# One row of w4 in a decode kernel: from the last POOL-queue load to four sync-queue loads on partitions 0 to 63

## The chip, the cores and the metric

The kernel runs on one core of a Trainium2 chip. The metric is the device time of one execution in microseconds: 211.09 us before the change, the median of three runs (210.95 to 211.11).

A core has five engines that run their own instruction streams: PE (TensorE, matmuls), DVE (VectorE), ACT (ScalarE), POOL (GpSimd) and SP (SyncE, which only issues DMAs here). Memory is moved by 16 DMA engines. A DMA that POOL issues goes through one queue, a DMA that SP issues through another; both queues are served by the same DMA engines. A load is cut into packets, and each DMA engine that takes part in a load signals its end.

## The reference

One decode step for four sequences (B = 4, one token each, D = 576) adds three things: the input `x`, attention over the last 2048 cached positions, and an MLP block. All inputs are bf16.

```python
xn = _layernorm(x)
out = x + attention(xn, k_cache, v_cache, wq, wo) + mlp(xn, w1, w2, w3, w4)

# attention: 32 query heads, 16 key heads, Dh 128, window W = 2048
q = (xn @ wq); scores = q k^T * Dh**-0.5; p = softmax(scores)
o = (p v) @ wo

# mlp, with one token per sequence: its shifted branch comes out as zero, so x1 = xn
h2 = gelu(_layernorm(x1) @ w3) @ w4          # w3 576 x 4608, w4 4608 x 576
mlp = x1 + h2
```

The branch through `w1` and `w2` shifts by one or two positions along a sequence of length one, so nothing but zeros is left of it; the kernel doesn't load those weights. What has to be read is mostly the cache: 16 loads of 4 MB (eight of K, eight of V), and about 20 MB of weights.

## The kernel before

**Loads.** `wq` comes first, on SP's queue, in two DMAs. All later big loads go through POOL's queue, in an order written out in `order` and issued by `flush_loads`: K and V tiles for eight head pairs (`load_kv`, indirect DMAs of 128 rows of 32 KB), `wo` in four quarters (`load_wo`), `w3` behind the second V tile, and at the very end the last quarter of `wo` and the whole of `w4` (`load_w4`). Three buffers hold K and V tiles; `free_one` issues the next load when a tile has been used up. `wq`, `w3` and `w4` follow one another in one buffer (tag "w", one buffer), so w4's tile can be written only after w3's last reader.

**Loop.** Each turn t of the main loop treats one pair of key heads: DVE turns the K tile (`k_transpose`, L297), PE makes scores (`k_scores`, L411), DVE and ACT do the softmax of the turn before, PE multiplies with V (`pv`, L475), and the head outputs are turned, summed and, every second turn, multiplied by a quarter of `wo` into the PSUM tile `acc` (`acc_matmuls`, L230). The program order of each engine is the order in the text of the kernel (`manual_schedule`).

**The MLP.** In turn t = 3 (`G_AT`) the first MLP product is made in between. `mlp_g(r)` for r = 0, 1, 2 multiplies the normalised input by column groups of w3 (L541) and copies the result from PSUM to SBUF (L545). The 4608 hidden values are kept as 36 columns of 128: hidden value e*2304 + p*18 + i stands on partition p in column e*18 + i. r = 0 and 1 make columns i = 0 to 15 of each half, r = 2 makes i = 16 and 17 of both. `mlp_turn(r)` brings the result to partitions with PE transposes (L554) and a DVE copy into `xs` (L560). `mlp_act` makes the tanh form of gelu on POOL and ACT (L564 to L569) and leaves it as bf16 in `gT`.

**The second MLP product.** w4 lies in the same way: partition p holds rows e*2304 + p*18 + i, 36 rows of 1,152 bytes. `load_w4` brings it in six pieces, `W4_PIECES = [0, 18, 25, 30, 34, 35, 36]`, that is 18, 7, 5, 4, 1 and 1 rows a partition. After the attention of the last head pair PE adds the pieces as they land, one pair of matmuls (two halves of 288 columns) for each row: the first two pieces into `acc` (L230), then the rest into two fresh PSUM tiles (`sum_open`, L244; `sum_matmuls`, L252), with the sum of `acc` added by `sum_fold` (L257). The result is cast by DVE (L719) and ACT (L721) and stored by SP (L722).

**PSUM tiles** of the pool `ps_m` (tag "m") rotate through two buffers: `g_ps` of r = 2, each `gT_ps`, the softmax sums `dn`, the spread heads `R` (read by ACT in `o_pick`, L521) and others take them in turn.

Of the kernel before, what the change touches and what calls it, by code (L numbers as in the profile page):

```python
# [22 lines left out]
def kernel(  # L23
# [14 lines left out]
    nc = tc.nc  # L38
    P = 128
    B, Sq, D = A_x.shape  # L40
# [4 lines left out]
    F = B_w3.shape[1]  # L45
# [3 lines left out]
    NF = F // P  # L49
    NFH = NF // 2  # L50
    NPR = Hkv // 2
    NJ = B * rep
    QD = 32
# [24 lines left out]
    wp = ctx.enter_context(tc.tile_pool(name="w", bufs=1))  # L78
# [4 lines left out]
    const = ctx.enter_context(tc.tile_pool(name="const", bufs=1))  # L83
# [3 lines left out]
    ps_m = ctx.enter_context(tc.tile_pool(name="ps_m", bufs=2, space=PSUM))  # L87
# [3 lines left out]
    w_tiles = {}  # L91
# [61 lines left out]
        nc.gpsimd.dma_start(out=t[:, KJ * F:], in_=B_w3[KJ * P:D, :].rearrange("r (e f) -> (r e) f", e=2))  # L153
        w_tiles["w3"] = t

    W4_PIECES = [0, NFH, NF - 11, NF - 6, NF - 2, NF - 1, NF]

    def load_w4():
        t = wp.tile([P, NF, D], BF16, tag="w", name="w4_sb")
        src = B_w4.rearrange("(e p i) n -> e p i n", e=2, p=P)  # L160
        for lo, hi in zip(W4_PIECES, W4_PIECES[1:]):
            e, at = divmod(lo, NFH)
            nc.gpsimd.dma_start(out=t[:, lo:hi, :], in_=src[e][:, at:at + hi - lo, :])  # L163
        w_tiles["w4"] = t

    order = [("K", 0), ("K", 1)]
    for t in range(NPR):
# [31 lines left out]
    ident_f = ident_w[:, 0:P]  # L199
# [15 lines left out]
    ln2T = cleared([P, KJ + 2, QD], "ln2T")  # L215
    ZP = (NSL - 1) * NJ
    qz = cleared([P, ZP + NPR * 4 * P], "qz")
    gT = const.tile([P, NF, B], BF16, name="gT")
    op = const.tile([P, WOR, B], BF16, name="op")

    acc = ps_acc.tile([P, CW], F32, name="acc")
# [5 lines left out]
    def acc_matmuls(terms):  # L227
        for k, (lhsT, rhs) in enumerate(terms):
            for i in range(NI):
                nc.tensor.matmul(out=acc_of(k % 2 * NI + i), lhsT=lhsT, rhs=rhs[:, i * CW:(i + 1) * CW],  # L230
                                 start=False, stop=False, skip_group_check=True)
# [17 lines left out]
    def sum_matmuls(terms, first=False):  # L249
        for k, (lhsT, rhs) in enumerate(terms):  # L250
            for i in range(NI):
                nc.tensor.matmul(out=sum_of(i), lhsT=lhsT, rhs=rhs[:, i * CW:(i + 1) * CW],  # L252
                                 start=first and k == 0, stop=False, skip_group_check=True)
# [48 lines left out]
    for kb in range(NQD):  # L302
        nc.gpsimd.tensor_copy(out=sel[:, :, :, kb, :],
                              in_=ident_bf[:].rearrange("p (ib i e) -> p ib e i", ib=2, e=2))
# [23 lines left out]
    for g in range(2):  # L328
        nc.gpsimd.tensor_copy(out=same_j[:, g * 2 * QD:(g + 1) * 2 * QD].rearrange("p (e s j) -> p e s j", e=2, j=NJ),
                              in_=sel_j[:].unsqueeze(2).to_broadcast([P, 2, NSL, NJ]))  # L330
# [177 lines left out]
    def o_spread(h):  # L508
        if h % WOQ < WOQ - 1:
            return  # L510
        x = st.pop("ox")
        R = ps_m.tile([P, B, WOR], F32, tag="m", name="R")
        for b in range(B):
            nc.tensor.matmul(out=R[:, b, :], lhsT=x[:, b].rearrange("p h d -> p (h d)"), rhs=sel_i[:],
                             start=True, stop=True)
        st["R"] = R
# [9 lines left out]
        acc_matmuls([(op[:, i, :], wo_tiles[h // WOQ][:, i, :]) for i in range(WOR)])  # L526

    G_CHUNKS = [(e, 4 * g, 4) for e in range(2) for g in range(NQD)] + [(e, 16, 2) for e in range(2)]
    xs = const.tile([P, NF, B], F32, name="g_x")
    g_sb = {}  # L530

    def mlp_g(r):
        w3 = w_tiles["w3"]
        chunks = G_CHUNKS[r * NQD:(r + 1) * NQD]
        n = chunks[0][2]
        g_ps = (ps_o if r < 2 else ps_m).tile([P, P, n], F32, tag="O" if r < 2 else "m", name="g_ps")
        for j in range(KJ + 1):
            for g, (e, i0, _) in enumerate(chunks):
                base, k = (j * F + e * (F // 2), j) if j < KJ else (KJ * F, KJ + e)
                cols = w3[:, base:base + F // 2].rearrange("p (q i) -> p q i", q=P)  # L540
                nc.tensor.matmul(out=g_ps[g * QD:(g + 1) * QD], lhsT=ln2T[:, k, :], rhs=cols[:, :, i0:i0 + n],  # L541
                                 start=(j == 0), stop=False, skip_group_check=True)
        m = len(chunks) * QD
        g_sb[r] = bigp.tile([P, P, n], F32, tag="g", name="g_sb", bufs=1)
        nc.scalar.activation(out=g_sb[r][0:m], in_=g_ps[0:m], func=ACT.Copy)  # L545

    def mlp_turn(r):
        chunks = G_CHUNKS[r * NQD:(r + 1) * NQD]
        n, m = chunks[0][2], len(chunks)
        gT_all = ps_m.tile([P, n * m, QD], F32, tag="m", name="gT_ps")  # L550
        gT_ps = gT_all[:].rearrange("p (u g) x -> p u g x", u=n)
        gs = g_sb.pop(r)
        for u in range(n):
            nc.tensor.transpose(out=gT_ps[:, u].rearrange("p g x -> p (g x)"), in_=gs[0:m * QD, :, u],  # L554
                                identity=ident_f[0:m * QD, 0:m * QD])
        if r < 2:
            dst = xs[:, r * NFH:r * NFH + 16, :].rearrange("p (g u) b -> p u g b", u=n)
        else:
            dst = xs[:].rearrange("p (g c) b -> p c g b", c=NFH)[:, 16:18]
        nc.vector.tensor_copy(out=dst, in_=gT_ps[:, :, :, 0:B])  # L560

    def mlp_act():
        u = const.tile([P, NF, B], F32, name="g_u")
        nc.gpsimd.tensor_tensor(out=u[:], in0=xs[:], in1=xs[:], op=ALU.mult)  # L564
        nc.gpsimd.tensor_scalar(out=u[:], in0=u[:], scalar1=GELU_A, scalar2=1.0, op0=ALU.mult, op1=ALU.add)
        nc.gpsimd.tensor_tensor(out=u[:], in0=u[:], in1=xs[:], op=ALU.mult)
        nc.scalar.activation(out=u[:], in_=u[:], func=ACT.Tanh, scale=GELU_C)
        nc.gpsimd.tensor_scalar(out=u[:], in0=u[:], scalar1=0.5, scalar2=0.5, op0=ALU.mult, op1=ALU.add)
        nc.gpsimd.tensor_tensor(out=gT[:], in0=u[:], in1=xs[:], op=ALU.mult)  # L569

    def mlp_terms(lo, hi):
        w4 = w_tiles["w4"]
        return [(gT[:, u, :], w4[:, u, :]) for u in range(lo, hi)]


    G_AT = 3
# [1 line left out]
    for t in range(NPR - 1):  # L578
        a, o = t - 1, t - 2
        if a >= 0:  # L580
            sm_max(a, 1)
        if o >= 0:
            o_scale(o)
        k_transpose(t, 1)
        if t == G_AT:
            mlp_g(0)
        k_mask(t, 0)
        k_scores(t, 0, 0)
        if a >= 0:
# [12 lines left out]
        k_scores(t, 1, 0)  # L602
        if o >= 0:
            o_turn(o)
        k_scores(t, 1, 1)
        if a >= 0:
            sm_turn(a, 0)
        if o >= 0:
            o_sum(o)
            o_expand(2 * o + 1)  # L610
        k_transpose(t, 3)
        free_one()
        if a >= 0:
            sm_turn(a, 1)
        if t == G_AT:
            mlp_g(2)
            mlp_turn(1)
        k_mask(t, 1)
        k_scores(t, 2, 0)
        if a >= 0:  # L620
            sm_den(a)
            sm_rec(a)
            pv(a, 0, 0, SC // 2)
        k_scores(t, 2, 1)
        sm_max(t, 0)
        if o >= 0:
            o_spread(2 * o + 1)
        if a >= 0:
            pv(a, 0, SC // 2, SC)
        if o >= 0:  # L630
            o_pick(2 * o + 1)
        if t == G_AT:
            mlp_turn(2)
            mlp_act()
        if t + 1 < NPR:
            k_transpose(t + 1, 0)
        k_scores(t, 3, 0)
        if a >= 0:
            pv(a, 1, 0, SC // 2)
        k_scores(t, 3, 1)  # L640
        if a >= 0:
            pv(a, 1, SC // 2, SC)
            free_one()
        if o >= 0:
            o_proj(2 * o + 1)
# [57 lines left out]
    o_sum(hl)  # L703
    o_expand(2 * hl + 1)
    o_spread(2 * hl + 1)
    acc_matmuls(mlp_terms(*W4_PIECES[0:2]))
    o_pick(2 * hl + 1)
    o_proj(2 * hl + 1)
    acc_matmuls(mlp_terms(*W4_PIECES[1:3]))
    half = sum_open()  # L710
    sum_matmuls(mlp_terms(*W4_PIECES[2:4]), first=True)
    sum_fold(half)
    sum_matmuls(mlp_terms(W4_PIECES[3], NF))

    fin = const.tile([B, D], out.dtype)
    for i in range(NI):
        dst = fin[:, i * CW:(i + 1) * CW]
# [35 lines left out]
```

## Time and profile before

| what | us |
|---|---|
| median of 3 runs | 211.09 (210.95 to 211.11) |
| the profiled execution, its own time | 210.85 |
| its span, first to last instruction | 209.1 |
| PE busy | 144.0 (69%) |
| DVE busy | 124.3 (59%) |
| POOL busy, ACT busy | 31.6, 28.5 |
| POOL's queue, time of its packets | 91.7% of 16 engines' span, 82.45 MB |
| SP's queue, time of its packets | 5.5%, 4.72 MB |

Issues and landings of the loads around the change:

```profile
w_sb<-in_B_w_dram POOLq DMA_DIRECT2D x1, 1008.0 KB, 30.6
w_sb<-in_B_w_dram POOLq DMA_DIRECT2D x1, 720.0 KB, 31.9
...
w_sb<-in_B_w_dram POOLq DMA_DIRECT2D x2, 144.0 KB, 28.6
```

Each line names the tile and the tensor, the issuing queue, how many DMAs, the size of one and the median microseconds from issue to landing. The two single-row pieces of w4 are the two of 144 KB.

The profile's "busy" counts what an engine executes. The chain of waits goes back from the last instruction: at each step to what released it, or to the instruction before it on the same engine. A DMA on that chain means that an engine stood waiting for data at that point. The trace also holds each DMA packet (queue, start, duration, size), and for each load the times at which DMA engines signalled its end.

### The profile page before, as it was taken

How to read it: one execution, taken by the hardware profiler on the slowest of the kernel's cores; microseconds unless marked ns; L12 is line 12 of the kernel's file. 1: busy time of each engine (PE TensorE's matmuls, PEld its weight loads, DVE VectorE, ACT ScalarE, POOL GpSimd, SP SyncE). 2: the span in 40 equal slices, each digit the busy share in tenths (PEclk: the TensorE clock that was granted, in tenths of full speed). 3: DMA queues.
4: the chain of work that ended last, by engine and by line, in shares of the span. 5: the costliest groups of instructions: out<-in, count | busy, mean ns of one | idle time of the engine just before them, and what ended most of it. 6: DMA issues, size and time to landing. Idle time of an engine off the chain costs nothing.

```text
span 209.1 us, 2165 instructions
## 1 busy us (share of the span) xinstructions
PE 144.0 (69%) x878; PEld 57.7 (28%) x878; DVE 124.3 (59%) x174; ACT 28.5 (14%) x64; POOL 31.6 (15%) x63
## 2 busy tenths in 40 slices
PE   0248198649669933069996793677959947986974
PEld 0013133223214310014432431133314312432442
DVE  5510679993199600098908991998099818896220
ACT  6102500100102011003001201020102010204010
POOL 5680001003200110000133011001010152100000
PEclk9999669997979995559999999696997995899699
DMA  8999999999999999999999999999999999999991
GB/s 302 401 439 464 401 433 429 464 401 433 470 397 437 447 429 407 407 471 445 407 442 453 401 439 423 464 401 439 464 401 428 442 433 407 445 451 404 420 404 60
DMA packets 4155, 87.32 MB, mean 418 GB/s; under 512 B 488, under 2 KB 496, under 8 KB 1200
## 3 DMA queue, kind: packets, MB, share of 16 engines
q0 software_dynamic: 3840, 82.45, 91.7%
q1 hardware_dynamic: 296, 4.72, 5.5%
q8 instruction: 7, 0.11, 0.2%
q14 instruction: 4, 0.03, 0.0%
q10 hardware_dynamic: 8, 0.00, 0.0%
HBM read 87.17 MB, written 0.00 MB: 417 GB/s over the span
## 4 chain that ended last, share of the span: by engine, by line
DMA 63%; PE 18%; DVE 14%; POOL 2%; issue 2%; ACT 0%; DVEq 0%; POOLq 0%
DMA kn<-in_A_k_cache_dram,row 47%; DMA w_sb<-in_B_w_dram 16%; PE S L411 10%; DVE kt L297 9%; PE O L475 6%; DVE mx L417 1%; POOL w_sb L163 1%; DVE pt L456 1%; PE sum L252 1%; PE S L399 0%; POOL vn L125 0%; PE oT L486 0%; DVE dm L420 0%; POOL rstd L268 0%; POOL wo_sb L147 0%
## 5 line engine op out<-in xcount | busy, mean ns | idle before, releaser
L297 DVE STREAM_TRANSPOSE kt<-kn 128x2048 int32<-128x2048 int32 x32 | 73.6, 2304 | 48.7 <-DMA kn<-in_A_k_cache_dram,row 46.1
L411 PE MATMUL S<-kt,qz 128*128 128x512 bf16 x256 | 78.1, 438 | 33.6 <-DVE kt L297 33.6
L411 PEld LDWEIGHTS <-qz 128*128 128x128 bf16 x256 | 23.5, 104 | 72.5 <-issue 55.8
L475 PE MATMUL O<-vn,pt 128*64 128x512 bf16 x256 | 36.4, 415 | 6.5 <-DMA vn<-in_A_v_cache_dram,row 5.3
L456 DVE STREAM_TRANSPOSE pt<-E 64x512 bf16<-64x512 bf16 x32 | 22.1, 690 | 1.2 <-ACT E L447 0.9
L125 POOL DMA_INDIRECT vn<-in_A_v_cache_dram,row x8 | 7.7, 960 | 92.9 <-DVE kt L297 88.4
L447 ACT ACTIVATE E<-S,bias 128x512 bf16<-128x512 f32 x16 | 10.9, 683 | 75.9 <-DVE bias L440 75.9
L475 PEld LDWEIGHTS <-pt 128*64 128x64 bf16 x256 | 13.5, 116 | 23.3 <-issue 13.9
L125 POOL DMA_INDIRECT kn<-in_A_k_cache_dram,row x8 | 7.9, 989 | 41.5 <-PE O L475 22.7
L480 ACT ACTIVATE O_sb<-O,rd 128x512 f32<-128x512 f32 x8 | 5.5, 688 | 54.5 <-PE O L475 54.5
L417 DVE TENSOR_REDUCE mx<-S 128x1 f32<-128x512 f32 x16 | 10.7, 667 | 0.1
L541 PE MATMUL g_ps<-w_sb,ln2T 128*32 128x512 bf16 (+1 forms) x50 | 5.3, 512 | 3.6 <-DMA w_sb<-in_B_w_dram 3.6
L399 PE MATMUL S<-negbig,ohT 4*128 4x512 bf16 x16 | 6.4, 398 | 0.0
L496 DVE TENSOR_REDUCE on<-oT 128x16 bf16<-128x128 f32 x8 | 2.3, 286 | 5.2 <-PE oT L486 5.1
L486 PE MATMUL oT<-ident_w,O_sb 128*128 128x128 f32 x32 | 5.1, 284 | 0.0
L355 PE MATMUL q_ps<-wq_sb,xnT 128*32 128x512 bf16 x40 | 4.4, 625 | 0.9 <-DMA wq_sb<-in_A_wq_dram 0.9
L486 PEld LDWEIGHTS oT<-ident_w,O_sb 128*128 128x128 f32 x32 | 4.3, 154 | 2.7 <-issue 1.1
L163 POOL DMA_DIRECT2D w_sb<-in_B_w_dram x6 | 3.3, 586 | 7.6 <-DMA vn<-in_A_v_cache_dram,row 7.6
L420 DVE TENSOR_SCALAR dm<-sel_g,mx 128x8 bf16<-128x8 bf16 x16 | 3.9, 242 | 0.6
L282 PE MATMUL tp<-ident_bf,first 4*128 4x4 bf16 x8 | 0.6, 173 | 5.1 <-DVE first L269 5.1
L373 DVE COPY first<-qT_ps 128x64 bf16<-128x64 bf16 x2 | 0.3, 186 | 6.3 <-PE qT_ps L370 6.3
L230 PE MATMUL acc<-first,ident_w 4*4 4x288 f32 x4 | 1.1, 657 | 4.1 <-POOL first L342 4.1
(103 smaller groups left out, 80.0 us busy)
## 6 DMA issues: line engine op xcount, KB each, us to landing
wo_sb<-in_A_wo_dram POOLq DMA_DIRECT2D x4, 1152.0 KB, 23.2
w_sb<-in_B_w_dram POOLq DMA_DIRECT2D x1, 4608.0 KB, 29.5
wq_sb<-in_A_wq_dram SPq DMA_DIRECT2D x1, 4096.0 KB, 13.9
w_sb<-in_B_w_dram POOLq DMA_DIRECT2D x1, 2592.0 KB, 28.8
w_sb<-in_B_w_dram POOLq DMA_DIRECT2D x2, 576.0 KB, 31.5
w_sb<-in_B_w_dram POOLq DMA_DIRECT2D x1, 1008.0 KB, 30.6
w_sb<-in_B_w_dram POOLq DMA_DIRECT2D x1, 720.0 KB, 31.9
wq_sb<-in_A_wq_dram SPq DMA_DIRECT2D x1, 512.0 KB, 3.4
```

Source lines behind the costliest of these rows:

```text
L125: nc.gpsimd.indirect_dma_start(tl[:].rearrange("p c d -> p (c d)"), None, k_rows if kind == "K" else v_rows, bass.IndirectOffsetOnAxis(ap= ...
L163: nc.gpsimd.dma_start(out=t[:, lo:hi, :], in_=src[e][:, at:at + hi - lo, :])
L297: nc.vector.transpose(out=kt[:], in_=src)
L399: nc.tensor.matmul(out=S_ps[t, u][:].rearrange("p (c k) -> p c k", k=QD), lhsT=ohT[:], rhs=negbig[:].unsqueeze(1).to_broadcast([B, SC, QD] ...
L411: nc.tensor.matmul(out=S_ps[t, u][:], lhsT=qz[:, z0:z0 + P], rhs=kt[:, ib, sl * SC:(sl + 1) * SC, e:2 * QD:2].rearrange("p c k -> p (c k)" ...
L417: nc.vector.reduce_max(out=mx[:], in_=S_ps[t, u][:], axis=AX.X)
L447: nc.scalar.activation(out=E[t, u][:].rearrange("p c k -> p (c k)"), in_=S_ps.pop((t, u))[:], func=ACT.Exp, scale=scale, bias=st["bias", t ...
L456: nc.vector.transpose(out=pts[t % 2 * NU + u][rows, :, e * QD:(e + 1) * QD], in_=e_in[rows])
L475: nc.tensor.matmul(out=O_ps[t][rows], lhsT=pts[t % 2 * NU + u][:, c, :], rhs=vn[:, u, :, c, :], start=(u == 0 and c < 2), stop=False, skip ...
L480: nc.scalar.activation(out=O_sb[t][:], in_=O_ps.pop(t)[:], func=ACT.Copy, scale=st.pop(("rd", t))[:, 0:1])
L486: nc.tensor.transpose(out=oT[:, s, :], in_=o[:, s, :], identity=ident_w[:, s * NJ:s * NJ + P])
L541: nc.tensor.matmul(out=g_ps[g * QD:(g + 1) * QD], lhsT=ln2T[:, k, :], rhs=cols[:, :, i0:i0 + n], start=(j == 0), stop=False, skip_group_ch ...
```

## The change

The last of w4's 36 rows per partition (e = 1, i = 17: 128 rows, 144 KB) leaves POOL's queue. `W4_PIECES` becomes `[0, 18, 25, 30, 34, 35]`, five pieces. The new `load_w4_low` takes the tile of w4 already in turn t = 3, behind `mlp_turn(2)`, and loads those 128 rows with four DMAs on SP. Each takes 32 rows, in the order 8 x 4, onto 32 partitions: 0 to 31 or 32 to 63, in column 35 or 36 of the tile, which has 37 columns now. So one row for each of 128 partitions becomes two rows for each of 64.

The matching hidden values have to stand on the same 64 partitions in the same order. ACT copies that column of `g_ps` in the new order into `g_low` (two ACT instructions), PE turns it with two transposes of its own into `low_ps`, and DVE copies it; the other three columns of r = 2 are turned by two transposes and copied by two DVE copies, where two transposes and one copy did all four columns before. Columns 35 and 36 of `xs` are cleared once by POOL. `mlp_act` works on 37 columns. Terms 35 and 36 are contracted over 64 partitions, and their four matmuls stand ahead of the first piece of w4; the last row's two matmuls at the end of the program go away.

```diff
-    W4_PIECES = [0, NFH, NF - 11, NF - 6, NF - 2, NF - 1, NF]
+    NFM = NF - 1
+    NLOW = 2
+    NFX = NFM + NLOW
+    PL = P // NLOW
+    W4_PIECES = [0, NFH, NFM - 10, NFM - 5, NFM - 1, NFM]
+
+    def low_order(ap):
+        return ap.rearrange("p (h q g) -> p h g q", h=2, q=4)
+
+    def load_w4_low():
+        t = wp.tile([P, NFX, D], BF16, tag="w", name="w4_sb")
+        src = B_w4[F // 2:F, :].rearrange("(k h q g i) n -> i k h g q n", k=NLOW, h=2, q=4, i=NFH)[NFH - 1]
+        for k in range(NLOW):
+            for h in range(2):
+                nc.sync.dma_start(out=t[h * PL // 2:(h + 1) * PL // 2, NFM + k, :], in_=src[k, h])
+        w_tiles["w4"] = t
 
     def load_w4():
-        t = wp.tile([P, NF, D], BF16, tag="w", name="w4_sb")
         src = B_w4.rearrange("(e p i) n -> e p i n", e=2, p=P)
         for lo, hi in zip(W4_PIECES, W4_PIECES[1:]):
             e, at = divmod(lo, NFH)
-            nc.gpsimd.dma_start(out=t[:, lo:hi, :], in_=src[e][:, at:at + hi - lo, :])
-        w_tiles["w4"] = t
+            nc.gpsimd.dma_start(out=w_tiles["w4"][:, lo:hi, :], in_=src[e][:, at:at + hi - lo, :])
...
+    xs = const.tile([P, NFX, B], F32, name="g_x")
+    nc.gpsimd.memset(xs[:, NFM:, :], 0.0)
+    g_low = const.tile([2 * QD, P], F32, name="g_low")
...
+        if r == 2:
+            rows = slice(QD, 2 * QD)
+            for k in range(NLOW):
+                part_k = slice(k * PL, (k + 1) * PL)
+                nc.scalar.activation(out=g_low[rows, part_k].rearrange("p (h g q) -> p h g q", h=2, q=4),
+                                     in_=low_order(g_ps[rows, part_k, 1]), func=ACT.Copy)
...
+        if r == 2:
+            gT_ps = ps_m.tile([P, 3, QD], F32, tag="m", name="gT_ps")
+            nc.tensor.transpose(out=gT_ps[:, 0:2].rearrange("p g x -> p (g x)"), in_=gs[0:2 * QD, :, 0],
+                                identity=ident_f[0:2 * QD, 0:2 * QD])
+            nc.tensor.transpose(out=gT_ps[:, 2], in_=gs[0:QD, :, 1], identity=ident_f[0:QD, 0:QD])
+            rows = slice(QD, 2 * QD)
+            low_ps = ps_m.tile([PL, NLOW, QD], F32, tag="m", name="low_ps")
+            for k in range(NLOW):
+                nc.tensor.transpose(out=low_ps[:, k], in_=g_low[rows, k * PL:(k + 1) * PL],
+                                    identity=ident_f[rows, rows])
+            nc.vector.tensor_copy(out=xs[:, NFH - 2:NFH, :], in_=gT_ps[:, 0:3:2, 0:B])
+            nc.vector.tensor_copy(out=xs[:, NFM - 1, :], in_=gT_ps[:, 1, 0:B])
+            nc.vector.tensor_copy(out=xs[0:PL, NFM:, :], in_=low_ps[:, :, 0:B])
+            return
...
-        return [(gT[:, u, :], w4[:, u, :]) for u in range(lo, hi)]
+        return [(gT[0:n, u, :], w4[0:n, u, :]) for u in range(lo, hi) for n in (P if u < NFM else PL,)]
...
             mlp_turn(2)
+            load_w4_low()
             mlp_act()
...
     o_spread(2 * hl + 1)
+    acc_matmuls(mlp_terms(NFM, NFX))
     acc_matmuls(mlp_terms(*W4_PIECES[0:2]))
...
-    sum_matmuls(mlp_terms(W4_PIECES[3], NF))
+    sum_matmuls(mlp_terms(W4_PIECES[3], NFM))
```

More of the change, by code (lines that the diff above doesn't have):

```diff
@@ L217 @@
     qz = cleared([P, ZP + NPR * 4 * P], "qz")
-    gT = const.tile([P, NF, B], BF16, name="gT")
+    gT = const.tile([P, NFX, B], BF16, name="gT")
     op = const.tile([P, WOR, B], BF16, name="op")
@@ L528 @@
     G_CHUNKS = [(e, 4 * g, 4) for e in range(2) for g in range(NQD)] + [(e, 16, 2) for e in range(2)]
-    xs = const.tile([P, NF, B], F32, name="g_x")
+    xs = const.tile([P, NFX, B], F32, name="g_x")
+    nc.gpsimd.memset(xs[:, NFM:, :], 0.0)
+    g_low = const.tile([2 * QD, P], F32, name="g_low")
     g_sb = {}
@@ L549, in mlp_turn @@
         n, m = chunks[0][2], len(chunks)
+        gs = g_sb.pop(r)
+        if r == 2:
[12 more added lines that the diff above has]
+            return
         gT_all = ps_m.tile([P, n * m, QD], F32, tag="m", name="gT_ps")
         gT_ps = gT_all[:].rearrange("p (u g) x -> p u g x", u=n)
-        gs = g_sb.pop(r)
         for u in range(n):
@@ L555, in mlp_turn @@
                                 identity=ident_f[0:m * QD, 0:m * QD])
[L556 to L560, printed above, removed]
+        nc.vector.tensor_copy(out=xs[:, r * NFH:r * NFH + 16, :].rearrange("p (g u) b -> p u g b", u=n),
+                              in_=gT_ps[:, :, :, 0:B])
     def mlp_act():
-        u = const.tile([P, NF, B], F32, name="g_u")
+        u = const.tile([P, NFX, B], F32, name="g_u")
         nc.gpsimd.tensor_tensor(out=u[:], in0=xs[:], in1=xs[:], op=ALU.mult)
```

## The prediction

> **What bounds the kernel now.** I read the strip of 40 slices first, then the chain that ended last, then the stretches of the tail, and last the trace's single records of DMA packets and of landing signals.
>
> ```profile
> span 209.1 us, 2165 instructions
> ...
> DMA  8999999999999999999999999999999999999991
> ...
> DMA packets 4155, 87.32 MB, mean 418 GB/s; under 512 B 488, under 2 KB 496, under 8 KB 1200
> ...
> DMA 63%; PE 18%; DVE 14%; POOL 2%; issue 2%; ACT 0%; DVEq 0%; POOLq 0%
> ```
>
> The 16 DMA engines are 90% busy or more in every slice but the first and the last; no compute engine is (PE has 69% of the span). So time is bytes through 16 engines, plus what follows the last byte. The end of the chain says which bytes:
>
> ```profile
> 170.99 1.56 POOL w_sb L163 x3
> 172.55 32.71 DMA w_sb<-in_B_w_dram
> 205.26 0.04 issue
> 205.31 1.07 PE sum L252 x12
> 206.38 0.43 DVE fin L719
> ```
>
> ```profile
> core 0: us, PE busy (x) PEld busy (x) DVE busy (x) ACT busy (x) POOL busy (x), PEclk, DMA share, GB/s
> ...
> 200.00:203.00 3.00, 1.93 (x64) 1.54 (x68) 0.97 (x2) 0.20 (x1) 0.00 (x0) 1.00 1.01 421
> 203.00:206.10 3.10, 2.56 (x44) 1.35 (x32) 0.00 (x0) 0.41 (x1) 0.00 (x0) 1.00 0.53 212
> 206.10:209.10 3.00, 0.23 (x2) 0.03 (x1) 0.45 (x1) 0.40 (x1) 0.00 (x0) 1.00 0.00 2
> ```
>
> The reader is to see that the DMA share falls to 0.53 before the last piece of w4 is in: some engines are done while others still carry it. The landing signals (one from each engine per load) say how many. For the last one-row load nine come at 204.14 to 204.73 and seven at 205.68 to 206.00. After 206.00 PE does that row's two matmuls, ends at 206.38, and the output leaves. Whatever moves the 206.00 moves the end by as much.
>
> **Why seven engines are late.** Every POOL load closes on each engine with a 4-byte signal packet, so the 16 engines can be followed by their offsets, which stay fixed to a few ns from load to load. They jump only where a packet of an instruction queue comes in: 16,384 B ones at 32.7, 70.0, 106.2, 128.0, 164.7, 196.7 and 204.9 us, each moving its engine back by 1.40 to 1.42 us (0.95 of its own, some 0.5 added to the next packet), and 8,192 B ones at 60.8, 113.2, 162.0 and 190.2, moving theirs by 0.84, 0.52, 0.55 and 0.83. The first six large ones hit six engines. The small ones hit three: one twice, at 60.8 and 190.2, together 1.67 us. I call that one A; it gives the very last signal, 206.00, and the next is at 205.84. The large one at 204.9 hit an engine that was done.
>
> Which engines are low? The sync-queue load of wq's main part gives two families. Eight engines ran all their eight 32,768 B packets at 1,213 ns; the other eight had at least one of 1,221 to 1,394 ns. In the first family is an engine that carried one row of x, traced packet by packet (x row ends 2.338, next packet from 2.340, wq from 3.588): it is A. x's load, with 4 rows outermost, left four data packets and four engine signals; a load with 128 outermost leaves 16. So few-row loads fall on the first family, as far as this one case shows; I call it low. Of the seven late engines five are high (hit at 32.7, 70.0, 106.2, 128.0, 164.7) and two are low: A and the one hit at 196.7, which ends at about 205.68.
>
> **The change, part by part.**
>
> *The row leaves POOL's queue.* Single-row pieces cost each engine two packets of 178 ns and a signal; in steady flow, where packets overlap by 3 ns, that is 0.356 us, and 205.65 to 206.00 (last signals of the two single-row loads) measures 0.35. All 16 engines save it. A POOL issue goes too: it stood at 181.32 after a 7.64 us wait on an earlier landing, and landed 24.7 us later; nothing gained there.
>
> *Four loads on SP.* Each has its source as 8 x 4 rows, so by the nearest row (x: 4 outermost, four engines) I take 8 engines with 4 rows each; the other end would be 16 engines with 2 rows each. On eight, each gets 16 packets of 1,152 B and four signals. x's and the output's 1,152 B packets took 48 ns where they didn't wait for a first byte: 16 x 45 + 4 x 6 = 744 ns. Low engines so have 0.744 - 0.356 = +0.39 us, high ones -0.36. On sixteen, 8 x 45 + 24 = 384 ns for 356: nothing.
>
> [...]
>
> *Do the small packets cost more by their place among POOL's big ones?* SP waits for the last read of w3 (L541, done by 100.43) and has nothing else queued until the output, so the loads run from about 101, each between 32 KB packets of 1.21 us. The lower bound is zero: at 14.31 to 14.80 sync-queue signals stand between POOL's packets, and these still take 1,213 to 1,220 ns. The upper bound is the 0.21 to 0.53 us that the packet behind each instruction fetch lost; times 16 that is 3.4 to 8.5 us. [...]
>
> *Compute at t = 3.*
>
> ```profile
> 105.54 0.45 PE L554 MATMUL gT_ps<-ident_w,g_sb 64*128 64x64 f32 x2
> ...
> 106.03 0.17 DVE L560 COPY g_x<-gT_ps 128x16 f32<-128x16 f32 x1 [1.51 <-PE gT_ps L554]
> ...
> 109.90 0.66 PE L230 MATMUL acc<-wo_sb,op 128*4 128x288 bf16 x16
> ...
> 110.25 1.00 POOL L125 DMA_INDIRECT kn<-in_A_k_cache_dram,row  x1 [1.22 <-PE O L475]
> 110.49 2.31 DVE L297 STREAM_TRANSPOSE kt<-kn 128x2048 int32<-128x2048 int32 x1 [4.29 <-DMA kn<-in_A_k_cache_dram,row]
> ```
>
> Two more transposes (+0.45 us PE by the two here), two more DVE copies (+0.34), two ACT copies (0.4 by L521's 0.20), 37 columns for 36 on POOL (2.04 us of work, +0.06). PE's next scores wait for the transpose that ends at 112.80, DVE stood idle 4.29 us, and the K load issued at 110.25 lands 19.8 us later behind a full queue. Without that cover it would be some 0.5 us. One POOL memset and the two further matmuls of the new head term (36 took 1.27 us at 201.25: +0.14 with one term moved there) lie before the wait for w4's third piece. All zero.
>
> *Later landings.* Low engines run 0.74 us later from some 125 us on. Until 190.2 A's offset is 0.99, so 1.73, the latest high engine's own: K and V land as before. At the tail the third and fourth pieces land at 203.88 + 0.74 = 204.62 and 206.00, the last at 206.39; PE keeps up.
>
> **Sum.** Last signal 206.00 - 0.36 + 0.74 = 206.39; span 209.1 + 0.39 = 209.49. The profiled execution took 210.85, 1.75 us around its span, and the median of the runs is 0.24 above it: 211.09 + 0.39 = **211.48**. The high engines' gain is real, and hidden behind A. Own range 211.25 to 211.75: the upper end if the large fetch of 204.9 comes up to a microsecond earlier (PE has eight more instructions before it) on a low engine not yet done, 204.73 + 0.39 + 1.41 = 206.53.
>
> **Rivals.**
>
> 1. *The late engines are all high in the changed kernel*, because instruction streams change (SP, ACT, DVE, PE) and the fetches of 190.2 and 196.7 fall elsewhere, or my families are the wrong way round for part of them. Then 205.84 - 0.36 = 205.48 ends it: -0.52, 210.57. For it: five of seven are high. Against: fetches follow each engine's own instruction count, and only a few instructions are added. A gone alone leaves the engine of 196.7: 205.68 + 0.39 = 206.07, 211.16.
>
> 2. *Each small packet breaks the flow of POOL's big ones.* One mechanism, at 101 to 125 us, on low engines: 16 breaks. It decides from 0.03 us a break (0.5 in all). At 0.21 it is 3.4 + 0.4, 214.9; at 0.53 about 220. For it: all eleven fetches cost such a break. Against: 14.3 us. [...]
>
> 3. *It doesn't concentrate*: the loads are split over 16 engines; +0.03, 211.12.
>
> **Chances.** Forecast 0.53, its sum just inside the bound; rival 1 in full 0.22, with A gone alone 0.07; rival 2 0.14; rival 3 0.04. A measurement of this kernel can tell about 0.2% (0.42 us) from no change. Of the forecast's 0.53 I put 0.29 over that bound (small costs of a hundredth of a microsecond per packet would do) and 0.24 within. Slower: 0.29 + 0.14 = 0.43. Faster: rival 1 in full, 0.22. Within: 0.24 + 0.07 + 0.04 = 0.35. The range takes rival 1 in and stops in rival 2's lowest part: 210.4 to 212.4.
>
> **What would show it.** In packet records of the changed kernel: sixteen 1,152 B packets on each of eight engines from about 101 us (eight engine signals for each load, not 16), with the 32 KB packets beside them at 1.213 us; offsets of one family growing by 0.74 us; fetches again at about 190 and 197; last signals of the last w4 piece near 206.4 from two engines and near 205.5 from five. In the chain: the same end, w_sb then L252. I am wrong if the latest signals come from engines without the new packets (rival 1), if packets beside the new ones stretch (rival 2), or if the stage at 110 to 130 us gets longer.

## The result and the profile after

The changed kernel takes 211.50 us (median of 16 runs, 211.23 to 211.72) beside 210.88 us for the kernel before in 16 runs of the same jobs: a ratio of 1.0025, 95% interval 1.0017 to 1.0032, slower by about 0.5 us. (The two medians lie 0.62 us apart.) Its profiled execution took 211.72 us, the longest of the 16; its span is 209.9 us, while the spans of the other 15 were 209.5 to 209.8. The kernel before had spans of 209.0 to 209.4 in nine runs of another job; elsewhere a few of its runs (four of 33, three of 18) took 212.2 to 212.3 us with spans of 210.3 to 210.5, and none of these was profiled.

The page and the end of the chain of waits, kernel after:

```profile
span 209.9 us, 2188 instructions
...
DMA packets 4267, 87.32 MB, mean 416 GB/s; under 512 B 504, under 2 KB 640, under 8 KB 1312
...
q0 software_dynamic: 3792, 82.30, 91.3%
q1 hardware_dynamic: 456, 4.87, 5.6%
```

```profile
170.75 1.56 POOL w_sb L177 x3
172.31 33.96 DMA w_sb<-in_B_w_dram
206.31 0.82 PE sum L265 x10
207.13 0.43 DVE fin L753
```

The bytes are the same, 87.32 MB. POOL's queue lost 48 packets, the 32 of 4,608 B and the 16 signals of the row; SP's gained 160, which is 128 rows and 32 signals. The issues of w4 come no later than before (170.75, before 170.99), yet the DMA that the chain ends with lasts 33.96 us where it lasted 32.71. So the loss is between issue and landing, not in front of the issue.

The stretches of the tail, kernel after (duration, busy time of each engine, granted clock, DMA share, GB/s):

```profile
200.00:203.00 3.00, 2.23 (x41) 1.40 (x44) 0.00 (x0) 0.00 (x0) 0.00 (x0) 0.66 1.01 423
203.00:206.10 3.10, 2.86 (x44) 1.60 (x37) 0.00 (x0) 0.41 (x1) 0.00 (x0) 0.78 0.61 248
206.10:207.10 1.00, 0.88 (x12) 0.35 (x9) 0.00 (x0) 0.00 (x0) 0.00 (x0) 1.00 0.00 0
```

PE's granted clock is lower than before up to 206.1 us (0.66 and 0.78 for 1.00), but PE still has to wait for the third and the fourth piece (204.94 and 206.31); behind 206.1, where PE's own work ends the chain, it is 1.00. The share of busy DMA engines still falls in the last three microseconds of the loads, to 0.61. The signals of the last one-row piece say who is late there:

| kernel | early engines | late engines | last two signals |
|---|---|---|---|
| before | nine, 204.14 to 204.73 | seven, 205.68 to 206.00 | 205.84, 206.00 |
| after | three at 204.09 to 204.32, four at 204.85 to 205.12 | seven, 205.40 to 205.73 | 206.47, 206.63 |

Three high engines that no instruction fetch hit stay where they were: the 0.36 us that they save is used up in this run by slower packets at 45 to 65 us, ahead of the change (the "stretch" of 0.35 us, defined below). Four low engines have come 0.8 us nearer to the late ones. The seven of the third column aren't the same seven as before: followed through the packet records, five are the high ones, and two are low ones that a small fetch had hit (112.7 and 162.0 us). Two engines are 0.7 us behind all others and set the end alone: A, and the low engine that the large fetch hits near 193 us in this run. Both are low, so the high engines' saving is of no use.

Turn 3, kernel after, single lines of the timeline:

```profile
100.82 3.00 SPq L170 DMA_DIRECT2D w_sb<-in_B_w_dram  x4
...
106.15 0.25 PE L580 MATMUL low_ps<-ident_w,g_low 32*64 32x32 f32 x2
...
106.64 0.15 DVE L584 COPY g_x<-low_ps 64x8 f32<-64x8 f32 x1
...
110.72 1.00 POOL L125 DMA_INDIRECT kn<-in_A_k_cache_dram,row  x1 [1.06 <-PE O L488]
110.78 2.31 DVE L310 STREAM_TRANSPOSE kt<-kn 128x2048 int32<-128x2048 int32 x1 [3.99 <-DMA kn<-in_A_k_cache_dram,row]
```

SP issues the four loads at once when w3 has been read. The added transposes and copies end well before DVE's transpose of the next K tile, which still waits 3.99 us for data. The next K load is issued 0.47 us later than before (110.72 for 110.25) and lands at 130.28 instead of 130.04, behind a full queue.

In the packet records the first of the four loads signals once at 102.04 and then eight times, from 109.41 to 110.48; the others likewise. The four loads left 128 packets of 1,152 B and 32 signal packets of 4 B, eight for each load. From about 105 to 128 us, beside the small packets, POOL's 32 KB packets keep 1,213 ns.

### The profile page after: what moved, and what is told of

The parts are those of the page before. It is cut to its first block, busy times and chain, and to the rows that moved or that the text cites. A ratio compares the mean times of both kernels' runs of the same rounds, so it can differ in the third digit from the quotient of the medians.

```text
span 209.9 us, 2188 instructions
## 1 busy us (share of the span) xinstructions
PE 143.2 (68%) x882; PEld 58.1 (28%) x882; DVE 124.3 (59%) x176; ACT 28.8 (14%) x66; POOL 31.2 (15%) x63
## 2 busy tenths in 40 slices
DMA packets 4267, 87.32 MB, mean 416 GB/s; under 512 B 504, under 2 KB 640, under 8 KB 1312
## 4 chain that ended last, share of the span: by engine, by line
DMA 65%; PE 16%; issue 8%; POOL 6%; DVE 3%; ACT 0%; POOLq 0%; DVEq 0%
DMA kn<-in_A_k_cache_dram,row 25%; DMA vn<-in_A_v_cache_dram,row 24%; DMA w_sb<-in_B_w_dram 16%; PE S L424 7%; PE O L488 5%; PE g_ps L556 1%; DVE kt L310 1%; POOL kn L125 1%; POOL w_sb L177 1%; PE gT_ps L589 1%; POOL first L355 1%; POOL wo_sb L147 1%; POOL rstd L281 1%; POOL vn L125 0%; POOL dup L292 0%
## 5 line engine op out<-in xcount | busy, mean ns | idle before, releaser
L488 PE MATMUL O<-vn,pt 128*64 128x512 bf16 x256 | 34.4, 396 | 6.6 <-DMA vn<-in_A_v_cache_dram,row 5.8
L243 PE MATMUL acc<-w_sb,gT 128*4 128x288 bf16 (+1 forms) x54 | 3.5, 406 | 1.9 <-DMA w_sb<-in_B_w_dram 1.9
L453 DVE TENSOR_SCALAR bias<-bp 128x1 f32<-128x1 f32 x8 | 1.3, 158 | 4.8 <-PE bp L448 4.8
```

The costliest lines, as they stand in the source:

```text
L488: nc.tensor.matmul(out=O_ps[t][rows], lhsT=pts[t % 2 * NU + u][:, c, :], rhs=vn[:, u, :, c, :], start=(u == 0 and c < 2), stop=False, skip ...
```

## The experiments

Ratios are to the kernel before in runs of the same jobs, with 95% intervals. "Stretch" below is worked out from the packet records: what the data packets of POOL's queue took over their usual duration, without the packets right behind a fetch, summed and divided by 16 engines. It is 0.04 us for the kernel before, and 0.35 us in the profiled run of the kernel after, nearly all of it at 45 to 65 us, ahead of anything that was changed.

**One early SP load of all 128 partitions.** The kernel before, with the row taken off POOL's queue and loaded early, but to where it was; no extra compute.

```diff
+    NFM = NF - 1
+    W4_PIECES = [0, NFH, NFM - 10, NFM - 5, NFM - 1, NFM]
+
+    def load_w4_row():
+        t = wp.tile([P, NF, D], BF16, tag="w", name="w4_sb")
+        nc.sync.dma_start(out=t[:, NFM, :], in_=B_w4.rearrange("(e p i) n -> e p i n", e=2, p=P)[1][:, NFH - 1, :])
+        w_tiles["w4"] = t
...
             mlp_turn(2)
+            load_w4_row()
             mlp_act()
...
+    acc_matmuls(mlp_terms(NFM, NF))
     acc_matmuls(mlp_terms(*W4_PIECES[0:2]))
...
-    sum_matmuls(mlp_terms(W4_PIECES[3], NF))
+    sum_matmuls(mlp_terms(W4_PIECES[3], NFM))
```

> The kernel before, with its last single row taken off POOL's queue and loaded in turn 3 by one SP load of all 128 partitions in the natural layout, added first in the tail as in the changed kernel; 36 columns, no extra compute. Theory (where the row goes is what counts: uneven work on the engines costs the changed kernel 0.4 to 0.5 us, and a stretch of the 32 KB packets, seen only where an engine writes partitions that another engine's big packets serve, costs the spread and the four-engine version): each engine writes the partitions that it serves in the 128-partition loads, so no stretched packets, 8 x 48 + 6 - 356 = +0.03 us on every engine; ratio 1.000 (0.9985 to 1.0015). Rival (being on SP's queue beside POOL's, or early, is the cost): stretched packets at about 101 to 112 us and a ratio of 1.0025 or more.

211.00 us, ratio 1.0002 (0.9987 to 1.0017). Stretch 0.06 us. The last signals are those of the kernel before: nine at 204.12 to 204.73, seven at 205.66 to 206.01. Neither the queue nor the time of the load costs anything that the interval can tell. The median is 0.13 us above the 210.87 of the same job, and the profile shows where 0.13 us come from: DVE's cast of the result starts at 206.50 in place of 206.37, although the last signals are the same. PE is the cause; the section on the prediction shows how.

**The same, with the changed kernel's compute in turn 3** (two ACT copies, two PE transposes and two DVE copies, whose result nothing uses).

```diff
...
+            for k in range(2):
+                part_k = slice(k * P // 2, (k + 1) * P // 2)
+                nc.scalar.activation(out=g_low[rows, part_k], in_=g_ps[rows, part_k, 1], func=ACT.Copy)
...
+            for k in range(2):
+                nc.tensor.transpose(out=low_ps[:, k], in_=g_low[rows, k * P // 2:(k + 1) * P // 2],
+                                    identity=ident_f[rows, rows])
+            nc.vector.tensor_copy(out=x_low[:, 0, :], in_=low_ps[:, 0, 0:B])
+            nc.vector.tensor_copy(out=x_low[:, 1, :], in_=low_ps[:, 1, 0:B])
```

> The same with the changed kernel's compute added in turn 3, its result unused: two ACT copies, two PE transposes, two DVE copies (columns 35 and 36 aren't made). Theory (that compute lies beside the wait for K): the same as without it, ratio 1.000 (0.9985 to 1.0015). Rival (it is the compute that costs): some 0.5 us more than without it, ratio 1.0025.

211.05 us, ratio 1.0001 (0.9981 to 1.0021). This compute is hidden. (The 37th column on POOL and one further pair of head matmuls, which the changed kernel also has, aren't in this version.) What is left to set the changed kernel apart from these two versions is which engines carry the row.

**The low loads twice, onto the same partitions.** To the changed kernel a second set of the four loads is added, into columns 0 and 1, which are overwritten later.

```diff
...
+        for k in range(NLOW):
+            for h in range(2):
+                nc.sync.dma_start(out=t[h * PL // 2:(h + 1) * PL // 2, k, :], in_=src[k, h])
```

> The changed kernel with its four SP loads issued once more onto the same partitions 0 to 63, into columns 0 and 1 of the tile, which POOL's later loads overwrite. Theory (the low engines' own work counts, and these writes stay on the partitions that each engine serves): no stretched packets, low engines +0.78 us, high engines unmoved, ratio 1.0062 (1.005 to 1.0075), clearly under the 1.0131 of the version that wrote partitions 64 to 127. Rival (twice as many small packets stretch the big ones whatever they write): 1.013.

212.40 us, ratio 1.0062 (1.0040 to 1.0083), stretch 0.06 us. The two late low engines signal last, at 206.96 and 207.16; three engines that no fetch hit stay at 204.00 to 204.24. So the time answers to the dose: 211.00 with the row on 16 engines, 211.50 with it on eight, 212.40 with twice that.

**The low loads twice, onto partitions 64 to 127**, into the unused half of columns 35 and 36.

```diff
...
+                nc.sync.dma_start(out=t[PL + h * PL // 2:PL + (h + 1) * PL // 2, NFM + k, :], in_=src[k, h])
```

> The changed kernel with the four SP loads issued once more, into the unused partitions 64 to 127 of the same two columns, again 8 x 4 rows each. Theory: the same eight engines carry 16 more packets of 48 ns and four signals, 0.79 us; the last signal and the time go up by 0.78 over the changed kernel, ratio to the kernel before 1.006 (1.005 to 1.007), and the high engines' last signals stay where they are. Rival (what counts is the bytes over all 16 engines): 147 KB at 416 GB/s is 0.35 us, ratio 1.004, and all engines move alike. If the engines went by the target's partitions, 64 to 127 would load the high engines: the low ones stay, the high ones come to 205.5 + 0.78 = 206.3, and the time stays at 1.0025.

213.75 us, ratio 1.0131 (1.0115 to 1.0146): more than the theory's 1.006. Here the three unhit engines came 1.2 us later too (205.29 to 205.53), and the stretch is 1.35 us, at 125 to 145 us, when the second set is in flight. The stretches of these two kernels, with the same bytes and engines:

```profile
125.00:145.00 20.00, 11.58 (x52) 4.36 (x50) 13.66 (x15) 2.13 (x5) 1.87 (x2) 0.83 1.00 398
```

```profile
125.00:145.00 20.00, 12.13 (x54) 4.55 (x52) 13.89 (x16) 2.13 (x5) 1.87 (x2) 0.79 0.99 423
```

The first line is the version that writes partitions 64 to 127, the second the one that writes 0 to 63. Both have DMA engines busy all the time (share 1.00 and 0.99), but the first moves 398 GB/s, the second 423. Busy engines that move less is how stretched packets look in this view.

**The second set shifted by 16 partitions.** The same bytes and packets as with both sets on partitions 0 to 63, but the second set goes onto partitions 16 to 47. I took it that other engines write these in the 128-partition loads; no record shows which engine writes which partition.

```diff
...
+                nc.sync.dma_start(out=t[16:48, 2 * k + h, :], in_=src[k, h])
```

> [...] Theory (writes onto another engine's partitions hold up both): 32 KB packets of 1.3 to 1.45 us while the second set is in flight, about 125 to 147 us, in sum some 0.5 to 1.5 us per engine, ratio 1.009 to 1.014. Rival (it was the partitions above 63, or the number of packets): the same ratio as with the unshifted set.

212.44 us, ratio 1.0073 (1.0053 to 1.0092), stretch 0.04 us: as without the shift. My theory, that any write onto another engine's partitions holds up both, isn't borne out: whatever engines write these partitions otherwise, the shift by 16 brought no stretch.

**The row spread over 16 engines.** As the changed kernel, with each load's 32 rows in plain order.

```diff
-        return ap.rearrange("p (h q g) -> p h g q", h=2, q=4)
+        return ap.rearrange("p (h g q) -> p h g q", h=2, q=4)
...
-        src = B_w4[F // 2:F, :].rearrange("(k h q g i) n -> i k h g q n", k=NLOW, h=2, q=4, i=NFH)[NFH - 1]
+        src = B_w4[F // 2:F, :].rearrange("(k h r i) n -> i k h r n", k=NLOW, h=2, i=NFH)[NFH - 1]
```

> The changed kernel, but each of the four SP loads takes its 32 rows in plain order (32 outermost, not 8 x 4), so that 16 engines carry two rows of each; columns 35 and 36, the two extra transposes, copies and matmuls stay. Theory (the loss is 0.78 us more work on eight engines, two of which are late at the end): per load 16 engine signals, no family falls back, every engine has 8 x 48 + 24 = 408 ns in place of 356; last signal at most 0.05 us above the kernel before, ratio 1.000 (0.9985 to 1.0010), about 0.5 us under the changed kernel. Rival a (small SP packets between POOL's big ones, or the added compute at t = 3, cost the time, wherever the rows go): it stays near 1.0025. Rival b (taking w4's last piece off POOL's queue is itself what costs): also 1.0025.

212.13 us, ratio 1.0054 (1.0040 to 1.0068): a miss, and the wrong way. Each load signals 16 times and no family falls back, as expected, but the stretch is 0.83 us, at 105 to 120 us and on all engines. The profiled execution, 212.74 us, is the longest of its five, the others taking 211.93 to 212.25: in it A was late from the start (the last signal of the first K load came at 24.01 us, the one before at 23.63) and alone at the end (207.68, the next at 206.76). This run first looked like a proof that the small packets themselves cost the time. The 128-partition load with its ratio of 1.0002 shows otherwise.

**The 128-partition load cut into four of 32 partitions.** The version with one early SP load, the same rows to the same places; what changes is how the rows are dealt out, 32 to a load, and there are three more signals for each engine.

```diff
-        nc.sync.dma_start(out=t[:, NFM, :], in_=B_w4.rearrange("(e p i) n -> e p i n", e=2, p=P)[1][:, NFH - 1, :])
+        src = B_w4.rearrange("(e p i) n -> e p i n", e=2, p=P)[1][:, NFH - 1, :]
+        for h in range(4):
+            nc.sync.dma_start(out=t[h * QD:(h + 1) * QD, NFM, :], in_=src[h * QD:(h + 1) * QD, :])
```

> The version with one early SP load of all 128 partitions (ratio 1.0002), the same rows to the same places, but in four SP loads of 32 partitions in plain order: 16 engines carry two rows of each load, so that engines of the low family also write partitions 64 to 127 and the high ones also 0 to 63. Work per engine is the same but for three more signals. Theory (an engine that writes the other half's partitions stretches everyone's big packets): stretched 32 KB packets on all engines while the loads are in flight, some 0.5 to 1 us in sum, ratio 1.003 to 1.006 as for the spread version. Rival (the stretch of the spread version came from the 64-partition layout or from its source order): none here, ratio 1.0005.

211.77 us, ratio 1.0049 (1.0024 to 1.0073), beside 1.0002 for one load. Its profiled execution took 213.17 us, the second longest of its 12 runs, so the stretch seen in it, 2.07 us, is more than the usual one. Half of it, 1.03 us, falls behind 120 us, when the last of the small packets (119.7 us) is through and all engines' 32 KB packets still take 1,359 ns; what does that isn't known. The other half, 1.01 us while the small packets run, is near the 0.9 us by which the medians differ (211.77 and 210.86). The stretches from 105 to 125 us, first with one load, then with four:

```profile
105.00:125.00 20.00, 17.01 (x113) 7.13 (x115) 14.20 (x19) 2.65 (x7) 4.61 (x8) 1.00 1.01 432
```

```profile
105.00:125.00 20.00, 16.54 (x101) 6.51 (x96) 13.52 (x17) 2.46 (x6) 4.61 (x8) 0.91 1.01 398
```

432 GB/s become 398 at the same share. In the four loads every engine writes into every quarter of the partitions, as all 16 signal for each load; which partitions an engine writes in the one load no record shows. The last section takes this up.

**The row on four engines.** Rows in the order 4 x 8.

```diff
-        return ap.rearrange("p (h q g) -> p h g q", h=2, q=4)
+        return ap.rearrange("p (h q g) -> p h g q", h=2, q=8)
...
-        src = B_w4[F // 2:F, :].rearrange("(k h q g i) n -> i k h g q n", k=NLOW, h=2, q=4, i=NFH)[NFH - 1]
+        src = B_w4[F // 2:F, :].rearrange("(k h q g i) n -> i k h g q n", k=NLOW, h=2, q=8, i=NFH)[NFH - 1]
...
-                nc.scalar.activation(out=g_low[rows, part_k].rearrange("p (h g q) -> p h g q", h=2, q=4),
+                nc.scalar.activation(out=g_low[rows, part_k].rearrange("p (h g q) -> p h g q", h=2, q=8),
```

> The changed kernel with the rows of each SP load in the order 4 x 8: four engines carry eight rows of each load, 32 packets of 48 ns in all, 1.56 us; against the kernel before +1.2 us on these four, -0.36 on the other twelve. Theory (few-row loads go to the first engines, and the twice-hit late engine A, which carried a row of x, is among the first four): five signals per load (one in advance and four), last signal 206.0 + 1.2 = 207.2, ratio 1.0057 (1.0045 to 1.007). Rival (A isn't among the first four): these end at about 205.9 at most, A at 205.64, ratio 0.999 to 1.000. If only the other late low engine is among them: 205.68 + 1.2 = 206.9, ratio 1.0042.

214.82 us, ratio 1.0183 (1.0162 to 1.0205), far over the 1.0057 expected. One engine is alone at the end: 209.91, the next at 208.70. In the packet records it is the engine that the small fetches of 60.7 and 190.1 us hit, and it carries 32 of the small packets: A is among the four. But the stretch is 2.77 us, at 110 to 140 us, and the sum can't be read from this run.

**Eight further loads of 16 rows.** To the changed kernel the same rows are added once more, in the order 4 x 4, onto partitions 0 to 15 and 32 to 47 (columns 0 to 3, overwritten later). On four engines that is 32 packets and eight signals more for each. I took these partitions to be the ones that the four write in the 128-partition loads too; no record shows that.

```diff
+        own = B_w4[F // 2:F, :].rearrange("(k h c q g i) n -> i k h c g q n", k=2, h=2, c=2, q=4, i=NFH)[NFH - 1]
...
+                    nc.sync.dma_start(out=t[h * QD:h * QD + 16, 2 * k + c, :], in_=own[k, h, c])
```

> [...] Theory (A is among the first four; no stretch where each engine writes its own): A +1.58 us over the changed kernel, ratio 1.010 (1.0085 to 1.0115). Rival (few engines with many small packets stretch the others' big packets by themselves, as in the version with four engines): stretched packets, 0.5 us or more on top, ratio 1.012 to 1.016.

213.03 us, ratio 1.0081 (1.0048 to 1.0115), stretch 0.15 us. The last signal is alone again, 208.14 with the next at 206.84, 1.5 us over the changed kernel's 206.63, for 1.58 expected. This agrees with A being among the four engines that such loads use, and the end follows it.

**Fewer DVE instructions.** 24 small ones moved off DVE in the changed kernel.

```diff
-        nc.vector.tensor_scalar(out=st["dm", t][:, u, :], in0=sel_g[:], scalar1=mx[:, 0:1], scalar2=None, op0=ALU.mult)
+        nc.gpsimd.tensor_scalar(out=st["dm", t][:, u, :], in0=sel_g[:], scalar1=mx[:, 0:1], scalar2=None, op0=ALU.mult)
...
-        nc.vector.tensor_scalar(out=bias[:], in0=st.pop(("bp", t))[:], scalar1=scale, scalar2=None, op0=ALU.mult)
+        nc.scalar.activation(out=bias[:], in_=st.pop(("bp", t))[:], func=ACT.Copy, scale=scale)
```

> The changed kernel with 24 of DVE's small instructions elsewhere: the 16 scalings of sel_g on POOL, the 8 bias scalings on ACT. Theory (the small fetches that hit A at about 61 and 187 to 190 are DVE's own instruction stream, the others POOL's and ACT's): the second one doesn't come before the end any more, A is 0.83 us earlier, and the end is set by the other late low engine, 0.16 us earlier; ratio 1.0018 (1.0005 to 1.003). Rival (they come by time or by another engine's stream): a small fetch near 187 to 190 is still there, nothing moves, 1.0025. If the moved instructions slow the softmax chain, the wait shows on the K stages and the ratio is above 1.003.

212.25 us, ratio 1.0051 (1.0035 to 1.0068). The fetch did what the theory says: the fourth small one, at 186.9 us in the kernel after, comes only at 212.3, behind the end, and two others come earlier (96.5 and 140.2, before 112.7 and 162.0). Only DVE has fewer instructions in this version, while POOL and ACT have more; the records don't name the engine that fetches. The time went the other way. One engine signals at 207.29, 1.5 us behind all others; in this run it had begun 0.95 us late in the first microseconds and then met the large fetch of 195.6. Whether that, or the moved instructions, makes the version slower isn't settled.

**The four loads on POOL.** `nc.gpsimd.dma_start` in place of `nc.sync.dma_start` in the changed kernel.

> The changed kernel with its four loads issued by POOL in place of SP, the same 8 x 4 rows onto partitions 0 to 63, behind the loads that POOL has issued by then. If POOL's few-row loads go to the same low eight engines as SP's, the low engines fall back by about 0.7 us (packets of four rows, 178 ns, four for each engine) and the time is near the changed kernel's (ratio 1.002 to 1.003). If POOL spreads each over 16 engines, or takes other engines for each load in turn, no family falls back as a whole: ratio 1.000 to 1.001, or more where 32 KB packets are stretched as in the spread version.

211.64 us, ratio 1.0015 (0.9980 to 1.0050): too wide to tell. No family falls back; the last signals are again nine and seven (204.62 to 205.47, 206.18 to 206.57), all some 0.5 us late, with a stretch of 0.60 us, most of it at 118 to 121 us, where the loads' own packets run (118.15 to 120.4).

## Why the prediction was right, point by point

**The forecast** was 211.48 us; the median is 211.50. That it agrees to 0.02 us is luck: the base of 211.09, the median of three runs, lies 0.21 above the 210.88 of the 16 runs beside the changed kernel, and the step is larger than the 0.39 of the sum, 0.5 us by the ratio and 0.62 by the medians. The direction and the mechanism are right, and two terms were too small: the small packets (0.42 for 0.39), and PE at the end (0.12 for zero).

**"Low engines so have +0.39 us."** Right, and a little more: followed through the records, the low engines fall back by 0.776 to 0.779 us against the high ones, for 0.744 in the sum. A small packet among big ones took 51 ns, not the 48 that I had taken from x and the output. That gives 0.42 for 0.39.

**"Eight engines with four rows each."** Shown by the eight later signals of each load, and it costs time: 1.0025, against 1.0002 for the row on 16 engines. Ahead of the change only x's load spoke for the eight, with four signals from its 4 rows.

**"Last signal 206.39."** Measured 206.63. The high engines came 0.25 us above their forecast too (205.73 for 205.48), by the stretch at 45 to 65 us in the one profiled run; without it the last signal is 206.38. In the other runs that stretch need not be there: their spans, 209.5 to 209.8, lie at or above the forecast 209.49.

**"PE keeps up."** Wrong, and with it the sentence that whatever moves the last signal moves the end by as much. The end of the kernel after, and of the version with one early 128-partition load:

```profile
206.31 0.78 PE L265 MATMUL sum<-w_sb,gT 128*4 128x288 bf16 x10
207.12 0.45 DVE L753 CAST fin<-sum 4x288 bf16<-4x288 f32 x1 [8.77 <-PE sum L265]
```

```profile
205.69 0.78 PE L257 MATMUL sum<-w_sb,gT 128*4 128x288 bf16 x10
206.50 0.45 DVE L726 CAST fin<-sum 4x288 bf16<-4x288 f32 x1 [5.93 <-PE sum L257]
```

Before, two single-row pieces followed the four-row piece, whose last signal came 0.74 us ahead of the end of the loads (205.26 and 206.00). Now one follows it, and the two land 0.36 us apart (206.27 and 206.63). PE takes some 0.12 us for the two matmuls of a row, so it is still at the four rows when the last one lands. Its ten matmuls run from 206.31 to 207.09 without a gap, and DVE starts 0.49 us behind the last signal in place of 0.37: 0.12 us that the sum had at nothing. The version with one early load has the last signals of the kernel before and the same 0.49 us (206.01 to 206.50). With 0.42 from the packets the sum is then 0.54, the span 209.64, and that is the middle of the other 15 spans.

Between the kernel after and the loads doubled onto the same partitions the medians differ by 0.9 us, for 0.78 worked out. There the end of the program takes longer: from the landing of the output to the last instruction it is 1.15 us in place of 0.92, which I put down to SP's four further loads; no run shows that by itself.

**The high engines' gain hidden behind A.** Shown by the last signals after the change, by the doubled loads (212.40 us beside 211.50), and by the eight further loads of 16 rows (213.03): what was put on A came out as time.

**No cost for the small packets' place.** The forecast left it at its lower bound, zero. Right for this kernel: no stretch at 105 to 128 us, where POOL's 32 KB packets took 1,213 ns. But the signals at 14.31 to 14.80 us, from which that bound came, don't speak for every load: loads on the same two queues did stretch the big packets in other versions, by 0.83 us in the spread version and by 1.35 us with the second set on partitions 64 to 127. That this change's order of rows, 8 x 4 onto partitions 0 to 63, stays clear of it was luck; no row from before the change could tell.

**Compute in turn 3 and the removed POOL issue at zero.** Right, 1.0001 with the compute; what PE does at the end is another matter (above).

**Rival 1** (all late engines high) fell: the fetches came at 186.9 and 193.3 us, 3.4 us earlier than before, on low engines again. **Rival 2** fell for this kernel: the low engines lost 0.78 us, with no break of 0.21 us at each small packet (3.4 us for 16). **Rival 3** fell by the signals. The fetch of 204.9 coming earlier on an unfinished engine didn't matter either; it came at 204.6, on a low engine that had just sent its last signal.

## What to carry to other kernels

In this kernel, bound by its DMA engines, the slowest one of them set the end, so look at the spread of the last signals before moving bytes: 0.36 us taken off the wrong engines was worth nothing, and 0.78 put on the one that is last was paid in full (212.40 us beside 211.50). A load on SP's queue need not be spread over all engines: for 32 rows in the order 8 x 4 eight engines signalled, for the same rows in plain order 16. Count the signals. Moving a small load to another queue and to an earlier time changed nothing in itself here that could be measured, with the DMA engines busy throughout (1.0002, interval 0.9987 to 1.0017). And look at what the compute engine has to do with the last pieces: here two of them land 0.36 us apart, and PE, which needs some 0.49 us for the four rows of the first, adds 0.12.

No version tried here beats the kernel before. A perfect balance of the last signals would be worth at most about 1.0 us, from 206.0 to the mean of the 16 signals near 205.0.

## What the runs showed of the hardware that was not expected

**Stretched packets.** In the spread version, in the four loads of 32 partitions, and in the second set onto partitions 64 to 127, the big packets of all 16 engines took longer while the small ones were in flight, by up to 0.19 us in the mean of a microsecond (1.40 us for 1.213 in the spread version). In the second set this made 398 GB/s of 423 at 125 to 145 us. None of it showed with one 128-partition load (stretch 0.06 us), with eight engines on partitions 0 to 63 (0.06 with both sets there), or with the second set shifted by 16 (0.04). My idea was that in the first three engines write the half of the partitions that they don't write in a 128-partition load; no record shows which engines write which half there, so that is an assumption. The pair of one load and four loads (1.0002 and 1.0049) would fit it. It doesn't fit the version with four engines, which stayed on partitions 0 to 63 and had the largest stretch, 2.77 us, while the eight further loads of 16 rows, on partitions 0 to 15 and 32 to 47, had 0.15. Nor does every stretch have to do with small packets: the kernel after has its 0.35 us at 45 to 65 us, where none is in flight, and half of the stretch in the profiled run of the four loads of 32 partitions comes behind the last of them. The cause is therefore open. What the two doubled sets show (1.0131 and 1.0062, the same number of small packets from the same number of engines) is that their number alone doesn't bring it. What differs is the partitions and the columns written, and the kernel after writes columns 35 and 36, those of the set that stretched, on partitions 0 to 63 without it.

**Instruction fetches.** In the kernel before a 16,384 B fetch moved its DMA engine back by 1.40 to 1.42 us and an 8,192 B one by 0.52 to 0.84 us, in a span in which the DMA engines are 90% busy or more in every slice but the first and the last. When A has its second small fetch goes with an instruction count: with 24 instructions fewer on DVE, and on no other engine, A had none before the end, and the fourth small fetch of the run came at 212.3 us in place of 186.9.

**Few-row loads on POOL's queue.** The four loads left 32 packets of 4,608 B and 32 of 16 B: by these counts an estimated eight engines with data and eight with 16 B for each load, and not the same eight each time, since no family fell back. Which engines they were is in no record.
